# A selection-attention and ReGLU kernel: q transposed together with its selection, batch 2 moved to DMA transposes, one layout per head pair in batch 1, and earlier weights

## The chip, the cores and the metric

The kernel runs on one core of a Trainium2 chip. The metric is device time in microseconds (us); lower is better. The kernel before takes 310.8 us.

The engines are TensorE (PE in the profile; PEld is its weight loading), VectorE (DVE), ScalarE (ACT), GpSimd (POOL) and SyncE (SP). Here SyncE only starts DMA transfers, and its queue is "SPq" in the profile. The program gives every engine a list of instructions, and the traces show the list being worked through in order (two runs with the same program, before and before_dma, have TensorE's 482 groups of like matmuls in the same order). So an instruction that has to wait holds up all that stand behind it on the same engine.

## The reference

Attention in four batches of eight heads, 768 tokens, head size 64. Keys are taken in chunks of 32; each query sees only the 6 chunks with the highest upper bound of the score. A ReGLU network follows.

```python
k_min, k_max = k_chunks.min(axis=3), k_chunks.max(axis=3)          # 24 chunks of 32 keys
ub = np.sum(np.maximum(q * k_min, q * k_max), axis=-1)             # upper bound by chunk, causal
top_chunks = np.argsort(ub, axis=-1)[..., -6:]
mask = chunk_of_key_is_in_top & causal
attn = softmax(where(mask, q @ k.T / 8, -1e9)) @ v
x = attn.reshape(3072, 512)
out = (np.maximum(x @ w_gate, 0) * (x @ w_val)) @ w_out            # 512 -> 1536 -> 512
```

## The kernel before

The work is cut into 16 jobs, four pairs of heads in each of the four batches (the code counts batches b = 0 to 3, the text 1 to 4), and the feed-forward network into six units of 512 tokens. A list scheduler in Python, `Plan`, simulates the engines with assumed costs and fixes the order of instructions on each engine before anything runs. Feed-forward work of one unit fills TensorE's gaps in the attention of the next batch.

A job loads k, q and v, casts them to bf16 on GpSimd, and turns k and q so that features lie on partitions. There are two ways to do that. Batches 1 and 2 load k and q in 2-KB rows and turn them on TensorE; batches 3 and 4 load them in 256-byte rows and have SyncE start a DMA transpose:

```python
WIDE   = lambda b: b < 2     # k, q loaded in 2-KB rows
PE_KQ  = lambda b: b < 2     # k, q turned on TensorE, not by DMA transpose
PE_SEL = lambda b: b < 2     # the selection likewise
PE_X   = lambda b: b < 2     # the attention output likewise

def turned(name, tag, src, nr, on_pe, prio, after, makes, hold, np_=128):
    if on_pe:
        ...                  # nr matmuls against the identity, result in PSUM
    else:
        def f():
            t = new(tag, name, [128, nr, 128], BF16)
            nc.sync.dma_start_transpose(out=t, in_=src())
        op("SP", 1.25, prio, f, ..., lag=2.6)     # the plan's costs: 1.25 of SyncE, landing 2.6 later
```

So a job of batches 3 and 4 puts at least four transposes (k, q, selection, output) on the same in-order queue of SyncE that also starts the loads of all later jobs:

```python
# job_front(j): loads, started four jobs ahead
nc.sync.dma_start(out=o.rearrange("p (h r d) -> p h r d", h=2, d=D),
                  in_=s.rearrange("h (r p) d -> p h r d", p=128))      # rows of 256 bytes
...
# job_sel(j): the selection 0/1 per (query, chunk), turned, and copied beside q
sT = turned(sn, ..., lambda: sel, nr, on_pe, p, [("sel", j)], [sn], [])
for h in range(2):
    copy_half(eng[h], nr * 128, p + 0.01, qx[1 - h][64 * h:64 * h + 64], sT, h, ...)
# job_scores(j): 64 feature rows of k and 64 rows of a chunk indicator in one matmul of 128 rows;
# the indicator rows add a large negative number where a chunk was not selected
nc.tensor.matmul(t[:, h, o:o + m * 128], kx[h][:, c * 128:(c + 1) * 128],
                 qx[h][:, (qb - 1) * 128:(qb - 1 + m) * 128], ...)
```

Weights come through GpSimd's queue: four groups of w_gate and w_val, then four of w_out, each asked for when a certain load has landed.

The softmax here doesn't subtract the row's maximum and nothing guards it: scores larger than these inputs give would overflow.

Of the kernel before, what the change touches and what calls it, by code (L numbers as in the profile page):

```python
# [153 lines left out]
def kernel(  # L154
# [20 lines left out]


    nc = tc.nc

    B, H, S, D = q.shape
    CH = 32  # L180
    NCH = S // CH
# [21 lines left out]

    WIDE = lambda b: b < 2
    WS = 8

    PE_KQ = lambda b: b < 2
    PE_SEL = lambda b: b < 2
    PE_X = lambda b: b < 2

# [3 lines left out]

    WG = 4
    NPG = NTI // WG
    CW = NPG * 128
    wg_sb = [wpool.tile([128, KT_, CW], BF16, name=f"wg{i}") for i in range(WG)]
    wv_sb = [wpool.tile([128, KT_, CW], BF16, name=f"wv{i}") for i in range(WG)]
    wo_sb = [wpool.tile([128, NPG, d_model], BF16, name=f"wo{i}") for i in range(WG)]  # L220
    wg_h = moe_w_gate.rearrange("(kt p) n -> p kt n", p=128)
# [8 lines left out]
    sgn = const.tile([128, 2, 1], BF16)  # L230
    NSEL = 3
    sel_l = [const.tile([128, NQ, 128], BF16, name=f"sel{i}") for i in range(NSEL)]
# [7 lines left out]
    NQX = 3  # L240
    qx_l = [[const.tile([128, SQ], BF16, name=f"qx{h}_{i}") for h in range(2)]
            for i in range(NQX)]

# [27 lines left out]
    rings = {tag: n for tag, (_, _, n) in {**TAGS, **PS}.items()}  # L271
    rings["dq"] = 3
    plan = Plan(rings, set(PS))
# [15 lines left out]
    def setup():  # L289
# [3 lines left out]
        def f_sgn():  # L293
            nc.vector.memset(sgn[:, 0], -1.0)
            nc.vector.memset(sgn[:, 1], 1.0)
        op("DVE", 0.12, -99, f_sgn, makes=[("kbd0", i) for i in range(HP)])
        for i, t in enumerate(sel_l):
            op("DVE", 0.4, -98, lambda t=t: nc.vector.memset(t, 0.0), makes=[("sel0", i)])
# [22 lines left out]
        def f_i2():  # L321
# [6 lines left out]
            after=["ident2"], makes=["ind"])  # L328
        for hp in range(HP):
            for h in range(2):  # L330
                g = 64 - 64 * h
                op("DVE", 0.37, -12 + 4 * hp, lambda o=kx_l[hp][h][g:g + 64], i=ind[g:g + 64]:
                   nc.vector.tensor_copy(out=o, in_=i), after=["ind"], makes=[("kx0", hp)])


    def turned(name, tag, src, nr, on_pe, prio, after, makes, hold, np_=128):

        if on_pe:
            def f():
                t = new(tag, name, [128, nr, np_], BF16)  # L340
                s = src()
                for r in range(nr):
                    nc.tensor.matmul(t[:, r, :], s[:, r, :], ident[0:np_, 0:np_],  # L343
                                     is_transpose=True, start=(r == 0), stop=(r == nr - 1))
            op("PE", 0.057 * nr, prio, f, after=list(after) + ["ident"], makes=makes,
               take=[(tag, name)], hold=hold)
        else:
            def f():
                t = new(tag, name, [128, nr, 128], BF16)
                nc.sync.dma_start_transpose(out=t, in_=src())  # L350
            op("SP", 1.25, prio, f, after=after, makes=makes, take=[(tag, name)], hold=hold,
               lag=2.6)
        if np_ < 128:
            return lambda: TL[name].rearrange("f s p -> f p s")
        return lambda: TL[name].rearrange("f r p -> f (r p)")

    def copy_half(eng, n, prio, out, src, h, after, makes, hold):
        def f():
            i = src()[64 * h:64 * h + 64]
            if eng == "ACT":  # L360
                nc.scalar.activation(out=out, in_=i, func=ACT.Copy)
            else:
                nc.vector.tensor_copy(out=out, in_=i)  # L363
        op(eng, act_cost(n) if eng == "ACT" else dve_cost(n), prio, f, after=after,
           makes=makes, hold=hold)
# [6 lines left out]
    def first_block(b):  # L372
        p0 = -30.0 + b
        src3 = (("k", k), ("q", q), ("v", v))
        for nm, src in src3:
            rn = (nm + "raw", "P", b)

            def f_ld(nm=nm, src=src, rn=rn):
                t = new(nm + "raw", rn)
                nc.sync.dma_start(out=t[:, 0:H * D].rearrange("p (h d) -> p h d", d=D),  # L380
                                  in_=src[b, :, 0:128].rearrange("h p d -> p h d"))
            op("SP", 0.6, -40.0 + b, f_ld, makes=[("iss", nm, b - B)],
               take=[(nm + "raw", rn), ("dq", ("dq", nm, b - B))], lag=0.0)
            op("DMA", 1.22, -40.0 + b, None, after=[("iss", nm, b - B)],
               makes=[("ld", nm, b - B)], hold=[rn, ("dq", nm, b - B)])
            if nm == "v":
# [81 lines left out]
    def job_front(j):  # L468
# [8 lines left out]
        for nm, src in (("k", k), ("q", q), ("v", v)):  # L477
# [8 lines left out]
            def f_ld(nm=nm, src=src, rn=rn, np_=np_, ns=ns, lo=lo, big=big):  # L486
# [9 lines left out]
                else:  # L496
                    o = o.rearrange("p (h r d) -> p h r d", h=2, d=D)
                    for h in range(2):
                        nc.sync.dma_start(out=o[:, h],
                                          in_=s[h].rearrange("(r p) d -> p r d", p=128))  # L500
            dq = [] if big else [("dq", nm, j, i) for i in range(2)]
            op("SP", 1.1 if lo and not big else 0.6, pL, f_ld, makes=[("iss", nm, j)],
# [17 lines left out]
            def f_cast(nm=nm, rn=rn, bn=bn, np_=np_, ns=ns):  # L520
# [4 lines left out]
            op("POOL", cost, pT - 0.1, f_cast, after=[("ld", nm, j)], makes=[bn],  # L525
               take=[(nm + "bf", bn)], hold=[rn])

        on_pe = PE_KQ(b)

# [27 lines left out]
        eng = ("DVE", "DVE") if on_pe else ("ACT", "DVE")  # L557
        for h in range(2):
            copy_half(eng[h], n, pT + 0.05, tok(kx[h][64 * h:64 * h + 64]), kT, h,
                      [kn] + [("s", i) for i in prev], [("kx", j)], [kn])  # L560
        kbd = kbd_l[hp]
        for h in range(2):
            def f_kbd(h=h):
                nc.vector.tensor_tensor(
                    out=kbd[64 * h:64 * h + 64, :, 1 - h], in0=TL[mm][64 * h:64 * h + 64],
                    in1=sgn[64 * h:64 * h + 64].to_broadcast([64, 2, NCH]), op=ALU.mult)
# [9 lines left out]

        for nm, e, o in (("qmn", "ACT" if on_pe else "DVE", -1.0),
                         ("qmx", "ACT" if on_pe else "DVE", 1.0)):
            def f_q(nm=nm, e=e, o=o):
# [7 lines left out]
               makes=[("qm", j)], take=[(nm, (nm, j))], hold=[qn])  # L587
        eng = ("ACT", "ACT") if on_pe else ("ACT", "DVE")
        for h in range(2):
            copy_half(eng[h], n, pT + 0.06, tok(qx[h][64 * h:64 * h + 64]), qT, h,  # L590
                      [qn, ("s", j - NQX)], [("qx", j)], [qn])

    def job_sel(j):
# [44 lines left out]

        sel = sel_l[j % NSEL]

        def f_lt():
            nc.vector.tensor_tensor(
                out=sel.rearrange("p r (h c) -> p r h c", h=2)[:, :, :, 0:NCH],
                in0=ub(), in1=TL[tn][:, :, :, KTOP - 1:KTOP].to_broadcast([128, nr, 2, NCH]),
                op=ALU.is_lt)
        op("DVE", 0.15 + 0.0013 * nr * 2 * NCH, p, f_lt,
           after=[tn, ("sel0", j % NSEL), ("selT", j - NSEL)], makes=[("sel", j)],
           hold=[uh, tn])
        sn = ("selT", j)
        on_pe = PE_SEL(b)  # L650
        sT = turned(sn, "T" if on_pe else "tT", lambda: sel, nr, on_pe, p,
                    [("sel", j)], [sn], [])
        qx = qx_l[j % NQX]
        eng = ("DVE", "DVE") if on_pe else ("DVE", "ACT")
        for h in range(2):
            copy_half(eng[h], nr * 128, p + 0.01, qx[1 - h][64 * h:64 * h + 64], sT, h,
                      [sn, ("s", j - NQX)], [("qx", j)], [sn])

    def job_scores(j):
# [5 lines left out]
        for bi, bank in enumerate(BANKS):  # L665
# [4 lines left out]
            def f_s(bank=bank, sn=sn):  # L670
                t = new("S", sn)
                for h in range(2):
                    o = 0
                    for si, (c, qb, m) in enumerate(bank):
                        nc.tensor.matmul(t[:, h, o:o + m * 128],  # L675
                                         kx[h][:, c * 128:(c + 1) * 128],
                                         qx[h][:, (qb - 1) * 128:(qb - 1 + m) * 128],
                                         start=(si == 0), stop=(si == len(bank) - 1))
                        o += m * 128
            op("PE", 2 * w / 2400.0 + 0.02, p, f_s, after=[("kx", j), ("qx", j), ("kx0", hp)],  # L680
               makes=[sn, ("s", j)], take=[("S", sn)])
# [96 lines left out]
    def s1(u, nt, p, wide):  # L778
        hn, xn = ("hT", u), ("xT", u)
        gi, gc = divmod(nt, NPG)  # L780
        cs = slice(gc * 128, (gc + 1) * 128)
# [63 lines left out]

    def weights(key, parts, prio, after):

# [3 lines left out]
        iss = ("wi",) + key  # L851
        op("POOL", 0.78 * len(parts), prio, f, after=after, makes=[iss], lag=0.0)
        op("SDMA", 2.7 * len(parts), prio, None, after=[iss], makes=[key])

# [4 lines left out]
    offs = {}  # L859
    for j in range(NJ):  # L860
        job_front(j)
        job_sel(j)
        offs[j] = job_scores(j)
        job_av(j, offs[j])
    for i in range(WG):
        weights(("w", i), [(wg_sb[i], wg_h[:, :, i * CW:(i + 1) * CW]),
                           (wv_sb[i], wv_h[:, :, i * CW:(i + 1) * CW])],
                (-28.0, -7.9, -7.8, -7.7)[i], [(("ld","v",-1),("ld","q",0),("ld","q",1),("ld","q",2))[i]])
    for i in range(WG):
        weights(("wo", i), [(wo_sb[i], wo_h[:, i * NPG:(i + 1) * NPG, :])],  # L870
                (4.0, 5.0, 6.0, 7.0)[i], [(("ld","v",3),("ld","v",3),("ld","v",3),("ld","v",3))[i]])

# [48 lines left out]
```

## Time and profile before

| | kernel before |
|---|---|
| median of 4 runs | 310.80 us (309.11 to 311.44) |
| profiled span | 308.1 us, mean granted clock 0.972 |
| busy | PE 274.3, VectorE 184.3, ScalarE 178.1, GpSimd 91.9 us |
| last attention matmul starts | 217.3 us; then 90.8 us of feed-forward only |

From the page, the span in 40 slices of 7.7 us. A digit is the busy share of a slice in tenths; PEclk is the granted clock, DMA the mean busy share of the 16 DMA engines.

```profile
PE   2841998967998998999999899999999999999994
PEclk9995899995999999999999999999999999999999
DMA  9999999999899779986662264231100110020002
```

TensorE is the limit from about 130 us to the end. It is not before: it waits around slices 3 and 4 and around slice 9, and its clock drops to a half after each of these waits. The DMA engines are full for the first ten slices and begin to have room at about 80 us.

The windows view of the kernel before, in three stretches: start and end, length, then busy us (and instructions) of PE, PEld, DVE, ACT and POOL, then granted clock, DMA share and GB/s.

```profile
0.00:80.00 80.00, 56.09 (x521) 32.29 (x530) 50.85 (x150) 39.69 (x53) 40.54 (x68) 0.89 1.20 210
80.00:200.00 120.00, 114.56 (x1128) 66.66 (x1146) 104.53 (x327) 99.09 (x131) 47.28 (x88) 1.00 0.72 139
200.00:308.10 108.10, 103.64 (x585) 49.53 (x593) 28.89 (x49) 39.30 (x60) 4.03 (x11) 1.00 0.12 41
```

TensorE is idle for 24 us of the first 80, but for only 5.4 us of the next 120. A DMA share above 1 is an artefact of overlapping records; read it as full.

The waits view names the transfers that it waited for (us in total, times, longest):

```profile
PE g L793 <- DMA wg_61<-in_moe_w_gate_dram: 6.0, 1, 6.0
PE yp L828 <- DMA wo_69<-in_moe_w_out_dram: 2.6, 1, 2.6
PE yp L828 <- DMA wo_70<-in_moe_w_out_dram: 2.2, 1, 2.2
```

The timeline of SyncE's queue, cut to six lines (start, length, queue, line, operation). The length is how long the instruction held the queue, not how long the transfer took. The time in which the queue waits for a producer is the pause before a line, as the 5.6 us before 107.04:

```profile
84.36 1.05 SPq L499 DMA_DIRECT2D qraw<-in_q_dram  x2
85.51 0.48 SPq L494 DMA_DIRECT2D vraw<-in_v_dram  x1
...
99.01 1.31 SPq L350 DMA_TRANSPOSE kT<-kbf  x1
100.38 1.06 SPq L494 DMA_DIRECT2D kraw<-in_k_dram  x1
107.04 0.94 SPq L499 DMA_DIRECT2D qraw<-in_q_dram  x2
108.03 1.21 SPq L350 DMA_TRANSPOSE qT<-qbf  x1
```

When nothing is in the way, a plain load holds the queue about 0.5 us and a transpose about 1.2 us.

### The profile page before, as it was taken

Reading aid. Unit: us, or ns where it says so; the run is one execution under the profiler, and the core shown is the slowest. Engines: PE = TensorE matmul, PEld = TensorE weight load, DVE = VectorE, ACT = ScalarE, POOL = GpSimd, SP = SyncE. Lnnn points to the kernel's source line nnn. Section 1 sums busy time; section 2 is a strip of 40 time slices with the busy share of each in tenths; the row PEclk is TensorE's granted clock in tenths of the full one; section 3 lists DMA queues with packets and bytes.
Section 4 is the critical chain, followed back from the end, with each engine's and each line's share of the span. In section 5 each row is a group of like instructions: output and inputs, shape, how many; then the busy total and the mean of one; then the engine's idle time right before and its main releaser. Section 6 shows DMA issues by size and latency. Waiting matters only on the chain.

```text
span 308.1 us, 5930 instructions
## 1 busy us (share of the span) xinstructions
PE 274.3 (89%) x2230; PEld 148.5 (48%) x2268; DVE 184.3 (60%) x524; ACT 178.1 (58%) x242; POOL 91.9 (30%) x164
## 2 busy tenths in 40 slices
PE   2841998967998998999999899999999999999994
PEld 1431455643565554555655455555544444444441
DVE  7454789952879999978998798523434023204310
ACT  3421378860979794877898788988233223233321
POOL 5594146670555263243533332223000000000000
PEclk9995899995999999999999999999999999999999
DMA  9999999999899779986662264231100110020002
GB/s 168 218 229 222 212 214 227 209 187 231 158 235 242 90 172 186 187 145 137 168 139 49 56 89 80 92 80 54 24 0 0 69 70 0 34 104 1 0 34 102
DMA packets 95389, 37.88 MB, mean 123 GB/s; under 512 B 83840, under 2 KB 89472, under 8 KB 95360
## 3 DMA queue, kind: packets, MB, share of 16 engines
q1 hardware_dynamic: 89536, 32.78, 53.5%
q0 software_dynamic: 5824, 4.72, 9.6%
q8 instruction: 17, 0.28, 0.4%
q14 instruction: 12, 0.10, 0.1%
HBM read 30.41 MB, written 6.29 MB: 119 GB/s over the span
## 4 chain that ended last, share of the span: by engine, by line
PE 58%; DMA 19%; POOL 6%; DVE 5%; issue 5%; ACT 3%; SPq 2%; POOLq 0%; ACTq 0%; DVEq 0%
PE g L793 20%; PE yp L828 19%; DMA vraw<-in_v_dram 7%; PE sT L675 7%; PE vl L793 6%; PE o L726 5%; DMA kraw<-in_k_dram 5%; DMA wo_70<-in_moe_w_out_dram 3%; DMA qT<-qbf 2%; DMA kT<-kbf 2%; POOL aT L698 2%; DVE kmm L552 1%; SPq L380 1%; ACT aT L686 1%; POOL kbf L521 1%
## 5 line engine op out<-in xcount | busy, mean ns | idle before, releaser
L686 ACT ACTIVATE aT<-sT 128x1024 bf16<-128x1024 f32 x80 | 78.7, 1022 | 20.7 <-PE sT L675 16.7
L804 ACT ACTIVATE grl<-g 128x512 bf16<-128x512 f32 x72 | 42.9, 596 | 58.5 <-PE g L793 50.3
L698 POOL TENSOR_SCALAR_AFFINE_SELECT aT<-aT 128x256 bf16<-128x256 bf16 x80 | 32.2, 417 | 63.5 <-ACT aT L686 63.1
L812 DVE TENSOR_TENSOR hT<-vl,grl 128x512 bf16<-128x512 f32 x48 | 33.1, 689 | 21.3 <-PE vl L793 20.2
L828 PEld LDWEIGHTS <-hT 128*128 128x128 bf16 x288 | 27.7, 99 | 37.2 <-issue 3.8
L812 DVE TENSOR_TENSOR hT<-g,grl 128x512 bf16<-128x512 f32 x24 | 16.6, 692 | 45.3 <-ACT grl L804 31.6
L552 DVE TENSOR_REDUCE kmm<-kT 128x24 bf16<-128x768 bf16 x32 | 29.8, 948 | 7.4 <-PE kT L343 7.2
L838 ACT ACTIVATE y<-yp 128x512 f32<-128x512 f32 x24 | 14.4, 598 | 27.3 <-PE yp L828 23.3
L675 PEld LDWEIGHTS <-kx_all 128*128 128x128 bf16 x256 | 21.5, 98 | 14.3 <-issue 1.3
L726 PEld LDWEIGHTS <-aT 128*128 128x128 bf16 x640 | 23.2, 98 | 9.3 <-POOL aT L698 2.7
L793 PE MATMUL g<-xT,wg_61 128*128 128x512 bf16 x69 | 18.5, 390 | 6.1 <-DMA wg_61<-in_moe_w_gate_dram 6.0
L828 PE MATMUL yp<-wo_69,hT 128*128 128x512 bf16 x71 | 19.9, 386 | 3.0 <-DMA wo_69<-in_moe_w_out_dram 2.6
L828 PE MATMUL yp<-wo_70,hT 128*128 128x512 bf16 x70 | 20.3, 400 | 2.2 <-DMA wo_70<-in_moe_w_out_dram 2.2
L828 PE MATMUL yp<-wo_71,hT 128*128 128x512 bf16 x70 | 19.2, 379 | 0.2
L828 PE MATMUL yp<-wo_72,hT 128*128 128x512 bf16 x70 | 19.0, 379 | 0.1
L793 PE MATMUL g<-xT,wg_63 128*128 128x512 bf16 x70 | 18.2, 379 | 0.9 <-ACT grl L804 0.8
L521 POOL CAST kbf<-kraw 96x1024 bf16<-96x1024 f32 (+1 forms) x16 | 15.2, 952 | 11.6 <-DMA kT<-kbf 5.1
L363 DVE COPY kx_all<-kT 64x768 bf16<-64x768 bf16 x24 | 18.2, 759 | 0.4
L793 PE MATMUL g<-xT,wg_62 128*128 128x512 bf16 x70 | 18.2, 379 | 0.2
L793 PE MATMUL g<-xT,wg_64 128*128 128x512 bf16 x69 | 18.2, 379 | 0.1
L521 POOL CAST qbf<-qraw 80x1024 bf16<-80x1024 f32 (+1 forms) x16 | 14.1, 882 | 13.4 <-DMA qT<-qbf 11.5
L741 DVE TENSOR_TENSOR x<-o,zr 128x320 bf16<-128x320 f32 x32 | 15.7, 491 | 1.1
(187 smaller groups left out, 449.7 us busy)
## 6 DMA issues: line engine op xcount, KB each, us to landing
kraw<-in_k_dram SPq DMA_DIRECT2D x16, 384.0 KB, 7.6
vraw<-in_v_dram SPq DMA_DIRECT2D x16, 384.0 KB, 6.4
out_dram<-y SPq DMA_DIRECT2D x24, 256.0 KB, 2.0
qraw<-in_q_dram SPq DMA_DIRECT2D x8, 320.0 KB, 12.2
qraw<-in_q_dram SPq DMA_DIRECT2D x16, 160.0 KB, 3.7
kraw<-in_k_dram SPq DMA_DIRECT2D x4, 256.0 KB, 5.0
qraw<-in_q_dram SPq DMA_DIRECT2D x4, 256.0 KB, 5.0
vraw<-in_v_dram SPq DMA_DIRECT2D x4, 256.0 KB, 5.1
```

The costliest lines, as they stand in the source:

```text
L363: nc.vector.tensor_copy(out=out, in_=i)
L521: nc.gpsimd.tensor_copy(out=new(nm + "bf", bn)[0:np_, 0:ns * 2 * D].rearrange("p (r h d) -> p r h d", h=2, d=D), in_=TL[rn][0:np_, 0:ns * ...
L552: nc.vector.tensor_reduce(out=TL[mm][:, m], in_=i, axis=AX.XY if wide else AX.X, op=o)
L675: nc.tensor.matmul(t[:, h, o:o + m * 128], kx[h][:, c * 128:(c + 1) * 128], qx[h][:, (qb - 1) * 128:(qb - 1 + m) * 128], start=(si == 0), ...
L686: nc.scalar.activation(out=TL[an][:, :, a0:a0 + w], in_=TL[sn][:, :, 0:w], func=ACT.Exp, scale=scale)
L698: nc.gpsimd.affine_select(out=d, in_=d, compare_op=ALU.is_ge, fill=0.0, base=0, channel_multiplier=-1, pattern=[[0, 2], [1, 128]])
L726: nc.tensor.matmul(TL[on][:, r - 1, h - h0, :], TL[an][:, h, o:o + 128], vb[:, h, c, :], start=(i == 0), stop=(i == NP - 1))
L741: nc.vector.tensor_tensor(out=TL[xn][:, :, h0 * D:(h0 + hs) * D].rearrange("p r (h d) -> p r h d", d=D), in0=TL[on][:, :, :, 0:D], in1=TL[ ...
L793: nc.tensor.matmul(ps, w[:, kt, cs], TL[xn][:, kt, :], start=(kt == 0), stop=(kt == KT_ - 1))
L804: nc.scalar.activation(out=new("grl", rn), in_=g, func=ACT.Relu)
L812: nc.vector.tensor_tensor(out=TL[hn][:, nt, :], in0=vv, in1=TL[rn], op=ALU.mult)
L828: nc.tensor.matmul(TL[pn], TL[hn][:, nt, tl * 128:(tl + 1) * 128], wo_sb[nt // NPG][:, nt % NPG, :], start=(nt == 0), stop=(nt == NTI - 1))
```

## The change

The change aims at TensorE's idle first 80 us, and at work that TensorE and VectorE need not do. It has four parts:

- **W** (weights): the first group of w_gate and w_val is smaller (groups of 2, 3, 3 and 4 columns of 128), all are asked for earlier, w_out comes in two halves, v loads of the first blocks are put back, and the plan allows more loads under way.
- **P** (pair): in batch 1 both heads of a pair share one layout, so that copies from PSUM become single copies of all 128 partitions; the scores become pairs of 64-row matmuls.
- **D** (DMA): batch 2 gives up its TensorE transposes and its 2-KB rows and is treated as batches 3 and 4.
- **J** (join): GpSimd casts q a second time, in token order, into a tile beside the selection; one DMA transpose of that tile delivers the score operand, where before the selection was transposed alone and four half copies followed.

The diff, cut to its core (comments after # are added here; "..." marks cuts):

```diff
@@ weights: four groups, the first smaller; w_out in two halves
-    WG = 4
-    NPG = NTI // WG
+    WGS = [2, 3, 3, 4]
+    NPG = NTI // 2                      # w_out's halves
-    rings["dq"] = 3
+    rings["dq"] = 6                     # loads that the plan lets be under way
@@ ... weights asked for when loads are issued, not when they have landed
-                (-28.0, -7.9, -7.8, -7.7)[i], [(("ld","v",-1),("ld","q",0),("ld","q",1),("ld","q",2))[i]])
+                (-28.0, ...)[i], [(("iss","v",-1),("iss","k",0),("iss","v",0),("iss","v",1))[i]], 1.5 if i == 0 else 3.5)
@@ batch 2 joins batches 3 and 4: 256-byte rows and DMA transposes
-    WIDE = lambda b: b < 2
+    WIDE = lambda b: b < 1
+    PAIR = lambda b: b < 1
-    PE_KQ = lambda b: b < 2
-    PE_SEL = lambda b: b < 2
-    PE_X = lambda b: b < 2
+    PE_KQ = lambda b: b < 1
+    PE_SEL = lambda b: b < 1
+    PE_X = lambda b: b < 1
@@ q and its selection side by side in token order, one tile
-    qx_l = [[const.tile([128, SQ], BF16, ...) for h in range(2)] for i in range(NQX)]
+    qx_l = [const.tile([128, NQ, 2, 128], BF16, name=f"qx{i}") for i in range(NQX)]
+    cb_l = [const.tile([128, NQ, 2, 128], BF16, name=f"cb{i}") for i in range(NCB)]
+            if nm == "q" and not PAIR(b):
+                def f_cb(cb=cb, rn=rn):                      # GpSimd, besides the cast to qbf
+                    for h in range(2):
+                        nc.gpsimd.tensor_copy(out=cb[:, :, h, h * D:h * D + D], in_=src[:, h])
@@ ... one transpose in place of two copies of qT, one transpose and two copies of selT
+            op("SP", 1.6, p, lambda: nc.sync.dma_start_transpose(
+                out=qx.rearrange("f r h p -> f (r h) p"),
+                in_=cb.rearrange("p r h c -> p (r h c)").rearrange("p (x c) -> p x c", c=128)),
+               after=[("sel", j), ("cbq", j), ("s", j - NQX)], makes=[("qx", j), ("cT", j)],
+               lag=2.6 + 0.7)
@@ batch 1: one layout for both heads of a pair, scores as pairs of 64-row matmuls
+                if PAIR(b):
+                    for k_, q_, first in ((kx[0], x[:, 0:SQ], True), (ind, x[:, SQ:], False)):
+                        for si, (c, qb, m) in enumerate(bank):
+                            for h in range(2):
+                                hs = slice(64 * h, 64 * h + 64)
+                                nc.tensor.matmul(t[:, h, o:o + m * 128],
+                                                 k_[hs, c * 128:(c + 1) * 128],
+                                                 q_[hs, (qb - 1) * 128:(qb - 1 + m) * 128], ...)
```

## The prediction

> **What bounds the kernel now.** Span 308.1 us, TensorE (PE) busy 274.3. By stretch (windows view): 0–30.2 us, PE 12.8 busy; 30.2–71.4, 35.0 of 41.2; 71.4–133.8, 58.4 of 62.4; 133.8–218, 82.3 of 84.2; 218–308, 85.8 of 90.1. So PE is the limit from about 130 us on. Before that it waits: 6.0 us for the first gate-weight group (asked for at 16.8 us, landed 12.9 us later, first FFN matmul at 30.2), 2.6 + 2.2 us for w_out near 70 us (waits view), and runs cold after both (granted clock 0.63 in 20–30, 0.66 in 70–80). DMA moves 187–212 GB/s until 134 us; VectorE is 85% busy in 71–134.
>
> **What the change does, costed.**
> 1. Weights: first group 2/3 as large, all asked for before the jobs' first kbf cast. Both tensors of the old first group took 15.4 us from the ask; two thirds of that from an ask at about 14 us gives 24–25 us (estimate): first FFN matmul about 5 us earlier, w_out no longer late. Cost: loads share the DMA engines with more weight traffic (the Trainium skill, "DMA: Bandwidth & Descriptors", section "Issuing engines are not separate DMA queues"; the trace agrees: weights take 13–19 us to land beside the loads).
> 2. Batch 2 loses 104 PE transposes (a job: kT 0.51, qT 0.45, xt 0.44, selT alike, drain included): about 5 us of PE.
> 3. Batch 1 scores: twice as many matmuls, of 64 rows, in pairs on both halves. The first-block scores, 8 such of 128 columns, took 0.40 us, as much as 4 full ones: pairs overlap, as the Trainium skill's "TensorEngine Tiling (Array Packing)", "Key Properties", says; it also says a mode switch drains. 40 switches, estimate 1–3 us of PE.
> 4. VectorE: batch 1 saves a 0.96 and a 0.48 us copy a job; batch 2 kx copies (1.92, now one of 0.36), sel copies (0.96), xT copies (about 1.1); batches 3 and 4 about 1.0 a job. About 25 us less of 184. ScalarE: about 13 less. GpSimd: about 10 more (q cast twice).
> 5. DMA: 20 more transposes in batch 2 where DMA is saturated, joined ones twice as large, batch-2 k and q loads in 256-byte rows instead of 2 KB. Estimate 25–35 us more DMA work, against 0.57 free in 134–218.
>
> **What lies on the critical path.** Early weights 5 us plus about 2 at w_out; PE work −5 +2; relief of VectorE in 71–134 perhaps 3, given back in part by transposes behind loads in the congested stage (kT and qT landings of 5 us are already in the chain at 112–130). The last 90 us (pure FFN) don't change. Sum about −10 us.
>
> **Predicted: 300.5 us**, 80% range 291.5 to 309. Faster by over 2%: 0.70; within 2%: 0.26; slower: 0.04.
>
> **What would show each step.** First FFN matmul (g) at 24–26 us, its DMA wait below 3; first yp at 61–66 instead of 71.4, no wait over 1 us for w_out; PE busy 268–273; VectorE 155–162, ScalarE 162–168, GpSimd 100–105; attention's last matmuls at about 208 instead of 218; FFN tail still 90 us.
>
> **What would make it wrong.** Job 0's k cast now stands behind all weight issues on GpSimd, its k load behind two q loads: if that slips to 30 us, PE, in order, gains nothing early. Transposes of batch 2 stuck in SP's queue behind stalled loads (issues stall up to 8.7 us now) would starve PE at 70–110. If the 64-row pairs don't overlap, PE gets 8.5 us more. Conversely, with both weight waits gone and the clock full, 290 is possible.

## More of the kernel before

All times quoted are medians of a kernel's runs, all in the fast state unless the text says otherwise; ratios use fast runs alone.

The DMA view gives the median time from the start of a transpose to its landing, the last number:

```profile
kT<-kbf SPq DMA_TRANSPOSE x8, 3.4
qT<-qbf SPq DMA_TRANSPOSE x8, 2.6
```

## The result, and the profile after

The changed kernel is correct and slower: 320.56 us (319.55 to 321.17, 4 runs). The ratio is 1.032, with a 95% interval of 1.027 to 1.037. Ratios in this document are the mean time of one kernel's fast runs over that of the other's of the same rounds, so they are not quite the ratio of the medians quoted. The medians of the kernel before differ a little (308.97 to 310.81 us), so each experiment is judged by its own ratio.

The same views of the changed kernel. The slices (7.9 us each):

```profile
PE   2937999999579759698969989999999999999995
PEclk9985999999869859889989999999999999999999
DMA  9999999999999999999889642142000020020002
```

The windows:

```profile
0.00:80.00 80.00, 65.35 (x660) 35.94 (x670) 51.55 (x162) 43.83 (x59) 41.99 (x75) 0.94 1.23 208
80.00:200.00 120.00, 100.07 (x898) 54.98 (x911) 80.77 (x256) 76.86 (x100) 51.22 (x100) 0.90 0.97 172
200.00:317.90 117.90, 113.31 (x638) 54.15 (x647) 30.91 (x61) 42.15 (x65) 5.14 (x13) 1.00 0.14 44
```

Two things happened. In the first 80 us TensorE is busy 65.35 us instead of 56.09: the early weights work as intended. In the next 120 us it is busy 100.07 instead of 114.56, at a mean clock of 0.90 instead of 1.00, while the DMA share rises from 0.72 to 0.97. The gain is 9.3 us and the loss 14.5 us. The last attention matmul starts at 227.1 us instead of 217.3, and from there both kernels take 90.8 us to the end. So the whole difference of the two spans, 9.8 us, has arisen by then. Batch 2's attention is not what ends later (its exponentials end at 136.1 us, 140.0 before); what falls behind is the feed-forward work that should fill its gaps: by 140 us the trace shows 213 feed-forward matmuls started, against 246 before (of 864; both traces lack some records). PEclk falls again in the middle of the span; each drop follows one or more waits. The Trainium skill, "TensorE: Matmul & The Clock Gate", section "HAM oscillation — how this bites in real kernels", says that waits for DMA which outlast a window of about 3.4 us put the clock back to its slow state. Here the waits for DMA were up to 3.6 us and the clock was 0.74 in 100 to 120 us, where it had been 1.00 before; but drops also followed waits of 2.6 and 2.3 us for ScalarE (before 132.2 and 162.9 us).

The waits view of TensorE no longer lists any weight. In its place:

```profile
PE sT L727 <- DMA qx_91<-cb_94: 5.1, 2, 3.6
PE sT L727 <- DMA qx_92<-cb_95: 3.9, 2, 3.6
```

These are joined transposes of batch 2 (and, for 1.5 of the 9.0 us, of batch 3), waited for by the score matmuls. The chain of work that ended last, between 82 and 115 us, its DMA pieces (start, length, what):

```profile
82.94 6.37 DMA qx_92<-cb_95
...
96.45 4.03 DMA vraw<-in_v_dram
100.48 4.11 DMA kT<-kbf
...
110.09 4.30 DMA qx_91<-cb_94
```

The chain runs through transfers here, while the chain of the kernel before runs through TensorE and VectorE in 83 to 109 us. SyncE's queue, at the time of the first of these waits:

```profile
82.94 2.78 SPq L690 DMA_TRANSPOSE qx_92<-cb_95  x1
...
87.20 3.53 SPq L362 DMA_TRANSPOSE qT<-qbf  x1
90.94 1.21 SPq L362 DMA_TRANSPOSE kT<-kbf  x1
92.19 1.42 SPq L514 DMA_DIRECT2D qraw<-in_q_dram  x2
93.74 1.23 SPq L362 DMA_TRANSPOSE qT<-qbf  x1
...
171.99 0.53 SPq L895 DMA_DIRECT2D out_dram<-y  x1
```

It goes from one instruction to the next: from 82 to 172 us no pause is longer than 0.45 us, while the kernel before has 14 pauses over 0.5 us there, 29.8 us in all. So in this stage the producers are ready whenever the changed kernel's queue reaches an entry, and the queue sets the pace. Some transposes hold it 2.8 or 3.5 us instead of 1.2. Added up over stretches of 20 us, instruction by instruction from the trace (plain transfers + transposes, in us held of 20):

| stretch | before | after |
|---|---|---|
| 60–80 | 18.8 + 0 | 12.2 + 5.2 |
| 80–100 | 11.0 + 1.0 | 7.0 + 11.3 |
| 100–120 | 4.3 + 6.6 | 4.9 + 13.8 |
| 120–140 | 8.4 + 3.3 | 5.4 + 13.3 |
| 140–160 | 2.5 + 10.6 | 5.6 + 13.1 |
| 160–180 | 0 + 12.5 | 4.0 + 14.5 |

Before, the queue is held 11 to 13 us of each 20 from 80 us on. After, it is held 17.4 to 18.7 us of each 20 for 120 us; the rest are the short steps from one instruction to the next. Landings of transposes lengthen too:

```profile
kT<-kbf SPq DMA_TRANSPOSE x12, 4.2
qT<-qbf SPq DMA_TRANSPOSE x12, 3.9
qx_91<-cb_94 SPq DMA_TRANSPOSE x4, 3.9
```

The plan had assumed 2.6 us (3.3 for the joined one).

### The profile page after: what moved, and what is told of

Same layout as the page of the kernel before. It is cut to its first block, busy times and chain, and to the rows that moved or that the text cites. A ratio compares the mean times of both kernels' runs of the same rounds, so it can differ in the third digit from the quotient of the medians.

```text
span 317.9 us, 5858 instructions
## 1 busy us (share of the span) xinstructions
PE 278.7 (88%) x2193; PEld 145.1 (46%) x2228; DVE 163.2 (51%) x478; ACT 162.8 (51%) x222; POOL 98.4 (31%) x186
## 2 busy tenths in 40 slices
DMA packets 124348, 42.59 MB, mean 134 GB/s; under 512 B 114208, under 2 KB 119840, under 8 KB 124320
## 4 chain that ended last, share of the span: by engine, by line
PE 61%; DMA 22%; SPq 5%; ACT 4%; DVE 3%; issue 2%; POOL 2%; ACTq 0%; DVEq 0%
PE g L846 23%; PE yp L881 15%; PE vl L846 9%; DMA kraw<-in_k_dram 6%; PE sT L727 6%; DMA kT<-kbf 6%; PE o L779 4%; DMA qx_91<-cb_94 3%; DMA qx_92<-cb_95 3%; DMA vraw<-in_v_dram 3%; ACT aT L739 2%; SPq L394 2%; PE sT L717 1%; DVE hT L865 1%; SPq L514 1%
## 5 line engine op out<-in xcount | busy, mean ns | idle before, releaser
L881 PE MATMUL yp<-wo_69,hT 128*128 128x512 bf16 x140 | 36.1, 390 | 0.2
L881 PE MATMUL yp<-wo_70,hT 128*128 128x512 bf16 x137 | 34.5, 382 | 0.5 <-issue 0.2
L727 PEld LDWEIGHTS <-kx_all 128*128 128x128 bf16 x192 | 17.2, 102 | 30.0 <-issue 17.9
L846 PE MATMUL g<-xT,wg_64 128*128 128x512 bf16 x92 | 24.6, 383 | 0.2
L536 POOL CAST kbf<-kraw 128x768 bf16<-128x768 f32 (+1 forms) x16 | 14.3, 895 | 25.9 <-DMA kT<-kbf 11.4
L727 PE MATMUL sT<-qx_92,kx_all 128*128 128x512 bf16 (+3 forms) x64 | 12.8, 334 | 9.1 <-ACT aT L739 5.2
L846 PE MATMUL g<-xT,wg_63 128*128 128x512 bf16 x69 | 19.0, 393 | 1.4 <-ACT grl L857 1.1
L536 POOL CAST qbf<-qraw 128x640 bf16<-128x640 f32 (+1 forms) x16 | 13.1, 821 | 17.6 <-DMA qraw<-in_q_dram 12.9
L846 PE MATMUL g<-xT,wg_62 128*128 128x512 bf16 x67 | 18.2, 379 | 0.3
L375 ACT ACTIVATE kx_all<-kT 64x768 bf16<-64x768 bf16 x12 | 10.1, 842 | 15.9 <-DMA kT<-kbf 15.9
L846 PE MATMUL vl<-xT,wv_68 128*128 128x512 bf16 x61 | 17.2, 396 | 0.2
L610 ACT ACTIVATE qmn<-qT 128x640 bf16<-128x640 bf16 x16 | 11.7, 734 | 10.3 <-DMA qT<-qbf 6.8
L727 PE MATMUL sT<-qx_91,kx_all 128*128 128x512 bf16 (+3 forms) x64 | 11.8, 316 | 5.1 <-DMA qx_91<-cb_94 5.1
```

The lines of the kernel that those rows point to most:

```text
L536: nc.gpsimd.tensor_copy(out=new(nm + "bf", bn)[0:np_, 0:ns * 2 * D].rearrange("p (r h d) -> p r h d", h=2, d=D), in_=TL[rn][0:np_, 0:ns * ...
L610: nc.scalar.activation(out=tok(t), in_=qT(), func=ACT.Relu, scale=o)
L727: nc.tensor.matmul(t[:, h, o:o + m * 128].rearrange("k (r p) -> k r p", p=128), kx[h][:, c * 128:(c + 1) * 128], qx[:, qb - 1:qb - 1 + m, ...
L846: nc.tensor.matmul(ps, w[:, kt, cs], TL[xn][:, kt, :], start=(kt == 0), stop=(kt == KT_ - 1))
L881: nc.tensor.matmul(TL[pn], TL[hn][:, nt, tl * 128:(tl + 1) * 128], wo_sb[nt // NPG][:, nt % NPG, :], start=(nt == 0), stop=(nt == NTI - 1))
```

## The experiments

18 kernels ran. All ran 3 rounds. The main theory and its rivals:

1. **D loses the time**, because batch 2's transposes queue up behind loads on SyncE while the DMA engines are full.
2. W loses it: weights asked for early delay the loads.
3. J loses it: twice as many bytes in a transpose, or the second cast on GpSimd.
4. P loses it: 64-row matmuls do not pay.
5. The rows of 256 bytes lose it, not the transposes.

A sixth was not named: the plan is built anew for each kernel, so a part that is changed can also change the order of work on every engine. The traces show where it did; it is said below where it matters.

### One part at a time

**w_only**: the kernel before with W.

```diff
-    WG = 4
+    WGS = [2, 3, 3, 4]
-    rings["dq"] = 3
+    rings["dq"] = 6
     ... (w_out in halves, earlier asks, as in the change)
```

> The kernel before with the weight part of the change alone (group sizes 2, 3, 3, 4, earlier asks, two w_out halves, the order of the first-block loads). Theory 1 (the loss is batch 2's move from PE to DMA transposes, while the DMA engines are saturated): this alone gains, about 302 us, first yp near 62 us instead of 71. Theory 2 (the join is the loss): the same, about 302. Theory 3 (the early weights push the loads of batches 1 and 2 back and the loss comes from there): about 316 or more.

Measured: 312.58 us, ratio 1.012 (1.005 to 1.019). TensorE is busy 61.6 us in 0 to 80 (56.1 before), but 50.8 in 80 to 140 (56.3 before): it gains 5.5 us and gives 5.5 back. Feed-forward unit 0 is done at 89.1 instead of 96.5 us, but batch 2's exponentials end at 140.5 instead of 140.0. What was done early was the filler work that TensorE had for the later gaps; the pace there is set by how fast batch 2 gets ready. So the early gain was real and not kept; that it was lost in this way is read from these times and not tested by itself. The main theory had expected about 302 us here: that was wrong.

**d_only**: the kernel before with D.

```diff
-    WIDE = lambda b: b < 2        # and PE_KQ, PE_SEL, PE_X
+    WIDE = lambda b: b < 1
```

> The kernel before with batch 2 handed to DMA transposes and 256-byte loads, as batches 3 and 4 have it, and nothing else. Theory 1: slower than before, 320 to 328 us, PE idle between 80 and 180 us. Theory 2 (join): within 2% of before, about 309, as there is no joined transpose in it. Theory 3: within 2% of before.

Measured: 319.65 us, ratio 1.034 (1.030 to 1.039). D alone costs as much as the whole change. TensorE is busy 46.4 us in 80 to 140, where it was 56.3 before, and SyncE's queue goes through 82 to 172 us with only one pause over 0.5 us (1.1), as in the changed kernel.

**no_move**: the changed kernel with batch 2 back on TensorE, in the pair layout (W + P + J).

```diff
-    WIDE = lambda b: b < 1        # and PAIR, PE_KQ, PE_SEL, PE_X
+    WIDE = lambda b: b < 2
```

> The changed kernel with batch 2 given back to PE (wide loads, PE transposes, one layout per pair in batches 1 and 2); weights early and join in batches 3 and 4 stay. Theory 1: faster than both kernels, about 299 us. Theory 2: the join is still in 8 of 12 jobs, so about two thirds of the loss stays: 311 or more. Theory 3: 315 or more.

Measured: 311.2 us, ratio 1.006 (1.001 to 1.012). Without D, 2.5 of the 3.2 per cent are gone. The theory had expected about 299 us, faster than both kernels: the rest of the change gains nothing either. The parts do not add up (1.2 for W, 3.4 for D, 0.8 for P and J below, 3.2 together). The run also shows how 64-row matmuls run. Its timeline of TensorE (start, length, line, operands):

```profile
51.16 0.39 PE L717 MATMUL sT<-qx,kx_all 64*128 64x512 bf16 x2
51.39 0.38 PE L717 MATMUL sT<-qx,ind 64*128 64x512 bf16 x2
51.60 0.38 PE L717 MATMUL sT<-qx,kx_all 64*128 64x512 bf16 x2
51.82 0.38 PE L717 MATMUL sT<-qx,ind 64*128 64x512 bf16 x2
```

Each line is two matmuls, one on each half of the rows, and the next pair starts 0.21 to 0.23 us later. So pairs do overlap, and twice the number of matmuls takes about the same time. In the chain, four such matmuls take 0.54 us where two full ones take 0.43, and twelve 0.55 where six take 0.44: about 0.1 us for each of the five banks of a job, so about 0.5 us a job. This agrees with the Trainium skill, "TensorEngine Tiling (Array Packing)", section "Key Properties", that tiles work independently; that the extra 0.1 us is the drain of which it speaks is not shown.

**pair_join**: the kernel before with P in batches 1 and 2 and J in 3 and 4.

```diff
 # the no_move kernel with the parts of W taken back:
-    WGS = [2, 3, 3, 4]
+    WG = 4
-    rings["dq"] = 6
+    rings["dq"] = 3
```

> The kernel before with one layout per pair in batches 1 and 2 and the join in batches 3 and 4, without the weight part and without the move of batch 2. The runs so far put the weight part at +1.2% and the weight part with this at +0.6%: if the parts add up, 0.6% faster than before, 307 to 309 us. If VectorE's relief is worth what I predicted (3 us or more): 303 to 306.

Measured: 312.15 us, ratio 1.008 (1.004 to 1.011). Both expectations (307 to 309, 303 to 306) were missed: VectorE's relief gained nothing that shows.

**join_only**: the kernel before with J in batches 3 and 4.

```diff
+    JOIN = lambda b: b >= 2
-            if nm == "q" and not PAIR(b):
+            if nm == "q" and JOIN(b):        # second cast of q, by GpSimd
```

> The kernel before with the join in batches 3 and 4 alone (batches 1 and 2 in the old layout on PE, old weight groups). These batches had slack on the DMA engines (0.34 to 0.67 busy), and VectorE and ScalarE lose about 1 us a job each. If that relief counts: 1 to 2% faster than both kernels, 304 to 307 us. If PE has other work to do meanwhile: within 0.5% of before.

Measured: 314.7 us, ratio 1.013 (1.007 to 1.020). The wait of the attention-value matmuls for GpSimd's masking, 1.6 us in the kernel before, is here

```profile
PE o L791 <- POOL aT L763: 4.3, 5, 1.5
```

and GpSimd is busy 19.8 us of 140 to 180 instead of 15.8, TensorE 35.4 instead of 38.4. GpSimd works in order as well, so that the second cast of q stands before the masking of an earlier job. That this is the cause is argued from these numbers; no run took the cast alone away. Neither expectation (1 to 2 per cent faster, or within 0.5 per cent) came true.

**no_join**: the changed kernel without J.

```diff
-            if nm == "q" and not PAIR(b):
+            if False:
     ... (selection transposed alone, q and selection copied in halves, as before)
```

> The changed kernel without the join: q's and the selection's own DMA transposes and four half copies, as batches 3 and 4 had before; early weights, pair layout and batch 2 on DMA stay. Theory 1: still slow, 317 to 325 us. Theory 2: fast, about 303. Theory 3: about 318.

Measured: 318.56 us, ratio 1.032 (1.027 to 1.038), but the result was wrong (relative error 0.084): batch 1 and the other batches used different blocks of the same tile for the chunk bounds, so that stale blocks stayed in it. The instructions are the same as in the mended version.

**no_join2**: the same with a tile of bounds of its own for batch 1.

```diff
-    kbd_l = [const.tile([128, 2, 2, NCH], BF16, ...) for i in range(HP)]
+    kbd_l = [const.tile([128, 2, 2, NCH], BF16, ...) for i in range(2 * HP)]
```

> The changed kernel without the join, as no_join, with a zeroed tile of its own for batch 1 so that the result is right; the same instructions otherwise. Theory: the join plays no part in the loss, so again 317 to 322 us.

Measured: correct, 319.05 us, ratio 1.031 (1.027 to 1.036), the same as with J (1.032). So rival 3 does not explain the loss of the changed kernel, although J alone, on the kernel before, costs 1.3 per cent.

### What it is about D

**narrow_only**: the kernel before with only the rows of batch 2's k and q cut to 256 bytes, still turned on TensorE.

```diff
-    WIDE = lambda b: b < 2
+    WIDE = lambda b: b < 1
```

> The kernel before, with batch 2's k and q loaded in 256-byte rows instead of 2 KB ones, and batch 2 still transposed on PE. The move of batch 2 alone cost 3.4%; this does the load half of it. If the 256-byte rows are what costs (DMA engines' time per packet): 317 us or more. If the 20 DMA transposes cost it: within 1% of before, 308 to 312 us.

Measured: 310.85 us, ratio 1.010 (0.997 to 1.023), unclear: four of the seven runs of the kernel before in this call were slow, which leaves three to compare with (the same holds for d_poolq, before_wide and w_wide). By the interval it is at most two thirds of D's loss: rows alone do not make it.

**d_poolq**: d_only, with the loads of batches 2 to 4 started by GpSimd, to free SyncE's queue for the transposes.

```diff
+                qu = nc.gpsimd if b else nc.sync
-                    nc.sync.dma_start(...)
+                    qu.dma_start(...)
```

> Batch 2 on DMA transposes in the kernel before (which cost 3.4%), with the plain q, k and v loads of batches 2 to 4 asked for by GpSimd, so that SP's queue holds only transposes, first loads and stores. The DMA engines get the same work. If transposes wait because SP's one queue is full and in order: most of the loss comes back, 309 to 313 us. If the DMA engines' throughput is the limit: 317 us or more (GpSimd pays about 0.75 us an ask, so it may be slower still).

Measured: 343.01 us. Two of the four runs, the profiled one among them, were slow; the two fast ones give 1.105 (1.084 to 1.126). GpSimd is busy 134.9 us instead of about 92; what limits this kernel was not taken apart. It says nothing about SyncE's queue.

**before_wide, w_wide, after_wide**: three kernels with all 256-byte loads of the jobs in contiguous rows of 1,280 or 1,536 bytes per partition instead. Tokens land in the wrong places, so the results are wrong; the instructions, their order on every engine, and the bytes are the same.

```diff
-                                      in_=s.rearrange("h (r p) d -> p h r d", p=128))
+                                      in_=s.rearrange("h (p r) d -> p h (r d)", p=128))
```

> The kernel before with every 256-byte-row load of the jobs (v of all batches, k and q of batches 3 and 4) read in rows of 1280 or 1536 bytes: same bytes, same instructions, a fifth to a sixth of the packets; tokens land in other places, so the result is wrong on purpose. If DMA throughput holds the first 100 us back: 2% or more faster, 300 to 304 us. If VectorE and the dependence chains hold it: within 1% of before.

> The weights-only kernel (1.2% slower than before) with the same wide rows, wrong on purpose too. If its early gain of 6 us at the end of batch 1 was lost to late batch-2 loads (DMA throughput): 298 to 303 us and at least 1% faster than the wide kernel before. If it was lost to VectorE's chains or to the order of work: still 1% slower than the wide kernel before.

> The changed kernel with all its 256-byte-row job loads read in rows of 1280 or 1536 bytes (same bytes and instructions, far fewer packets; wrong result on purpose). If batch 2's transposes starve PE because the DMA engines are full of small packets: DMA landings of kT, qT and the joined one fall towards 2.6 us and the time to 308 us or less. If the transposes' own length and SP's in-order queue are what costs: 315 us or more.

Measured: before_wide 308.11 us, ratio 1.004 (0.987 to 1.021), unclear (one of its runs was slow; it is in the median and left out of the ratio); w_wide 309.61 us, 1.005 (0.995 to 1.015), unclear; after_wide 309.59 us, 0.999 (0.994 to 1.004). So wide rows give the changed kernel its whole loss back, and give the kernel before nothing that can be seen. w_wide is not faster than before_wide, so it does not show that W's gain was lost to late loads; the intervals are too wide for more. The windows of after_wide:

```profile
0.00:80.00 80.00, 63.72 (x618) 34.32 (x618) 52.01 (x146) 41.09 (x55) 41.65 (x73) 0.91 0.99 206
80.00:200.00 120.00, 110.61 (x1060) 61.89 (x1059) 86.78 (x289) 85.79 (x112) 53.91 (x106) 0.97 0.83 182
```

TensorE has 110.61 us in the middle stretch, against 100.07 in the changed kernel. The same 42.59 MB moved in 76,220 packets instead of 124,348. In the first 80 us the rate was the same (206 and 208 GB/s) at a DMA share of 0.99 instead of 1.23. That fits the Trainium skill, "DMA: Bandwidth & Descriptors", section "Specifications", which puts the smallest transfer for full rate at 512 bytes: the changed kernel has 114,208 packets under that, this one 55,840. SyncE's queue and the landings in after_wide:

```profile
82.83 1.35 SPq L690 DMA_TRANSPOSE qx<-cb  x1
...
160.85 0.54 SPq L895 DMA_DIRECT2D out_dram<-y  x1
```

```profile
kT<-kbf SPq DMA_TRANSPOSE x12, 4.6
qT<-qbf SPq DMA_TRANSPOSE x12, 4.1
qx<-cb SPq DMA_TRANSPOSE x12, 4.1
```

The transposes land no sooner than in the changed kernel, and yet the time is back. So the latency of a transpose is not what is lost, and neither of the two expectations fits. What differs is when a transfer gets its turn. SyncE's order is the same in both kernels, so the queue can be compared entry by entry. In the first 60 us it is held 19.3 us, against 56.3 in the changed kernel, and loads come early; but that lead is not kept, since batch 2's first transpose starts at 68.1 us, after a pause of 21 us, and in the changed kernel at 63.7. At 82.8 and 82.9 us both kernels stand at the same joined transpose. The 73 entries from there to the same store (160.85 above, 171.99 in the changed kernel) take 78.0 us here and 89.1 there, without a pause over 0.45 us in either. That is 11.0 of the 11.1 us by which the two spans differ (306.8 and 317.9). The queue is as full in one as in the other, but its entries let go sooner: the 35 transposes hold it 51.5 us instead of 57.9, and the 38 plain transfers 20.3 instead of 24.9. Batch 2's exponentials end at 128.0 us instead of 136.1.

**after_lag**: the changed kernel, with a plan that assumes 2 us more until a transpose has landed.

```diff
-               lag=2.6)           # and 2.6 + 0.7 for the joined one
+               lag=4.6)
```

> The changed kernel, its schedule built with 4.6 us assumed from a transpose's issue to its landing instead of 2.6 (measured: 3.6 to 4.2 median); no work changes, only the order of the instructions on each engine. If the loss is a static order that asks too early for late transposes: 305 to 312 us. If the stage has too little throughput: within 1% of the changed kernel, 317 to 323.

Measured: 320.86 us, ratio 1.037 (1.033 to 1.041). A plan with a truer latency, which puts much of the work in another order, is no better. It agrees with after_wide that the latency is not the point.

**after_pex**: the changed kernel with the attention output of batch 2 turned on TensorE, as before; 8 transposes fewer on SyncE.

```diff
-    PE_X = lambda b: b < 1
+    PE_X = lambda b: b < 2
```

> The changed kernel with the transposes of x of batch 2 back on PE (8 of batch 2's 20 DMA transposes, about 2.5 us of SP's queue a job; 20 PE transposes more). If SP's queue time is the limit in 80 to 180 us: a third or more of the loss comes back, 313 to 316 us. If it is the DMA engines' throughput: about a fifth of the bytes added, so 318 or so. If VectorE were the limit (it gets the copies back): no gain, 320 or more.

Measured: 317.26 us, ratio 1.024 (1.021 to 1.028). Taking 8 of the 20 added transposes (the output's, which few wait for at once) off the queue gives back 0.8 of the 3.2 per cent: less than the third that was expected if the queue is the limit, and near the 318 us that was expected if DMA throughput is.

**before_sp**: the kernel before, with three tiny loads (1 KB each, into a scratch tile) on SyncE at each of the 20 places where D would put a transpose, behind the same producers. TensorE still does the transposes, so that nothing waits for these loads.

```diff
+        if JOBS[j][0] == 1:
+            tiny(j, prio_of(j, "T"), [("kbf", j)])
+            tiny(j, prio_of(j, "T") + 0.03, [("qbf", j)])
+            tiny(j, prio_of(j, "U"), [("sel", j)])
+            tiny(j, prio_of(j, "X"), [("x", j)])
+            tiny(j, prio_of(j, "X"), [("x", j)])
```

> The kernel before, with three loads of 1 KB each on SP's queue in the places where each of batch 2's 20 transposes would stand (60 in all, about 1.2 us of SP's time per place), behind the same producers; next to no bytes; the result is right. If SP's in-order queue is what the transposes cost: 316 to 320 us. If the DMA engines' time is: within 1% of before, 308 to 312.

Measured: 320.45 us, ratio 1.035 (1.031 to 1.038). SyncE's timeline and the middle window:

```profile
104.33 1.48 SPq L600 DMA_DIRECT2D scr<-in_q_dram  x3
```

```profile
80.00:200.00 120.00, 104.63 (x1018) 61.20 (x1034) 94.16 (x287) 87.25 (x114) 41.81 (x77) 0.96 0.68 132
```

A group of three holds the queue about as long as one transpose, and moves 60 KB in all. The DMA share of the middle stretch is even lower than in the kernel before (0.68, 0.72), and still TensorE loses 9.9 us there. Batch 3's first transpose gets its turn at 101.56 us instead of 99.01, and TensorE then waits 5.1 us for ScalarE, which waits for that transpose. One thing was not held fixed: the plan was built with the new entries, and from about 150 us on the order of work on the other engines differs in places (64 of TensorE's 482 groups of matmuls). Up to there the order is that of the kernel before, and TensorE is already 6.2 us late. So time on SyncE's queue in these places, behind these producers, is enough by itself for a loss of about 6 us; in the rest the new order may share.

**before_dma**: the kernel before, with 16 extra loads of 192 KB in 256-byte rows into a scratch tile in batch 2: DMA traffic, with 16 issues on SyncE instead of 60.

```diff
+        if JOBS[j][0] == 1:
+            more(j, prio_of(j, "T"), [("kbf", j)])         # 4 a job
+            ...
```

> The kernel before with four more loads of 192 KB in 256-byte rows a job in batch 2 (3.1 MB in all, what the 20 transposes move or somewhat more), into a scratch nobody reads, behind the same producers. If the DMA engines' time is what the transposes cost: 315 us or more. If SP's queue is (16 issues of some 0.4 to 1 us against 20 of 1.2 to 3.5): 310 to 313.

Measured: 316.15 us, ratio 1.021 (1.017 to 1.025). The order of work on the other engines is that of the kernel before throughout. Batch 3's first transpose gets its turn at 103.11 us, and TensorE waits 5.4 us behind it, as in before_sp. The 16 loads held the queue nearly as much as the 60 tiny ones did (49.3 us of 80 to 140, against 50.7 in before_sp and 34.5 before), so this run does not show traffic apart from the queue.

**after_actv, before_actv**: the v loads of batches 2, 3 and 4 (12 loads) started by ScalarE's queue, everything else and the planned order as they were.

```diff
+                    eng = nc.scalar if nm == "v" and b >= 1 else nc.sync
-                    nc.sync.dma_start(out=o.rearrange("p (h r d) -> p h r d", h=2, d=D),
+                    eng.dma_start(out=o.rearrange("p (h r d) -> p h r d", h=2, d=D),
```

> The changed kernel with one word altered: the v loads of the jobs of batches 2, 3 and 4 (12 loads) are issued by ScalarE's queue instead of SyncE's; the planned order of every engine stays. Theory (SyncE's queue time starves the changed kernel between 80 and 190 us): the 12 loads hold SyncE at least 0.6 us each and up to 8 us when stalled, so the share of SyncE held in 60 to 120 us falls, attention ends earlier by 3 to 8 us, ratio to before 1.005 to 1.02 (the changed kernel had 1.03). Rival (it is the DMA engines' traffic that delays the transposes, and the queue's holding is only a symptom): same bytes, same rows, so the ratio stays 1.03 or above. A third outcome: ScalarE itself is held by stalled issues as SyncE was, its exponentials come late, and the ratio rises above 1.04 with ScalarE named in the waits; then the run says nothing on the rival.

> The kernel before with the same one alteration. Theory: SyncE holds its queue full only until about 105 us there and TensorE's limits after 134 us are its own work, so little changes: ratio 0.985 to 1.005. If ScalarE is held by the stalled issues: above 1.01. It is also the version most likely to beat the kernel before.

Measured: after_actv 318.84 us, ratio 1.026 (1.020 to 1.032); before_actv 318.57 us, 1.023 (1.015 to 1.032; one of its four runs was slow, the median of the other three is 317.72). Both expectations of the theory fail: the first is above the 1.005 to 1.02 that was named, with an interval that takes in both the theory's upper end and the changed kernel's ratio; the second should have stayed below 1.005. ScalarE was hardly held; its queue in after_actv:

```profile
93.73 0.39 ACTq L510 DMA_DIRECT2D vraw<-in_v_dram  x1
```

But SyncE's queue filled up again: in 80 to 160 us it was held 73.9 us, against 74.3 in the changed kernel. A queue without pauses is held all the time whatever stands in it, so the pace has to be looked at. Between the two entries used for after_wide, nine v loads were gone; the stretch took 84.8 us instead of 89.1, and the queue was 4.0 us ahead at its end. The 29 plain transfers left there held it 22.5 us, more each (0.78) than the 38 of the changed kernel (0.66). So the number of entries counts, and how fast the DMA engines take them counts as well. This fits the first half of what the Trainium skill, "DMA: Bandwidth & Descriptors", section "Issuing engines are not separate DMA queues", says, that transfers interleave on the same 16 engines whoever starts them. The lead was lost again: a kT transpose that started at 165.3 us, 2.6 us earlier than in the changed kernel, landed at 171.3, only 0.6 us earlier, and TensorE waited 4.6 us behind it; why it took 6.0 us was not taken apart. In before_actv the loads of batch 2 ran ahead, SyncE was held only 1.0 us of 60 to 80 (18.8 before), and w_out came late: TensorE waited 6.0 us for it, against 4.8 before, and its first w_out matmul came at 72.0 (68.4 before), stopping again for 1.6 us before 75.05. Batch 2's exponentials ended at 149.9 us instead of 140.0. Here the early loads for the attention lost more than they gained; that the late weights are the reason is read from these times.

## Why the prediction was wrong

The prediction said 300.5 us (291.5 to 309) and "faster by over 2%" at 0.70. It was 320.56 us, slower by 3.2 per cent, to which it had given 0.04. Point by point:

| predicted | measured | |
|---|---|---|
| first FFN matmul (g) at 24–26 us | 26.5 (30.2 before) | just outside |
| its DMA wait below 3 us | no such wait | right |
| first yp at 61–66 | 61.5 (68.4 before; the 71.4 of the prediction is the second w_out group's) | right |
| no wait over 1 us for w_out | none | right |
| PE busy 268–273 | 278.7 | wrong: the clock was 0.946 instead of 0.972; from these, about 34 us instead of 17 ran at half clock, which can add up to about 8 us (estimate) |
| VectorE 155–162, ScalarE 162–168, GpSimd 100–105 | 163.2, 162.8, 98.4 | just outside, right, just outside |
| 64-row pairs overlap, 1–3 us in all | they do; about 0.5 us a job, so 2 us | right |
| attention's last matmuls at about 208 | 227.1 (217.3 before) | wrong by 19 us |
| FFN tail still 90 us | 90.8, as before | right |

The removed and added work was counted well on every engine but one. Three terms of the sum failed:

1. **"5. DMA: 20 more transposes in batch 2 ..."** This was costed as work of the DMA engines alone, and held against the free DMA share of 134 to 218 us. Batch 2's scores run from about 90 to 140 us, and its operands are made from about 70 us on, where there was less room, and the transposes also need time on SyncE's queue: 20 × 1.2 us at best, behind loads in the same order. This is the step that failed: the path had SyncE's queue in it, and the sum did not. The critical-path sum gave it no number ("given back in part by transposes behind loads"). Measured, D alone costs 3.4 per cent, about 10 us; from 82 to 172 us the queue goes on without a pause over 0.45 us, where it had paused 29.8 us before, and TensorE waits 9.0 us for joined transposes, 7.5 of them in batch 2. The paragraph on what would make it wrong named this, "Transposes of batch 2 stuck in SP's queue behind stalled loads ... would starve PE at 70–110", and then gave it next to no weight in the range (0.04 for any slower result).
2. **"Early weights 5 us plus about 2 at w_out"** was counted as time kept. W made TensorE 5.5 us busier in the first 80 us and cost the same 5.5 us in 80 to 140, since it spent the filler work early; the whole of W was 1.2 per cent slower.
3. **"relief of VectorE in 71–134 perhaps 3"** did not come. VectorE is busy 21 us less over the span, but in the middle stretch batch 2's operands come from SyncE and the DMA engines, and VectorE has 80.77 us of work in 120 us there.

What is shown of the cause: D makes the loss (d_only, no_move). J does not (no_join2), narrow rows alone do not (narrow_only), a transpose's latency does not (after_wide, after_lag). The changed kernel's new order of work does not either: after_wide has the same order on every engine and loses nothing. From 82 to 172 us SyncE's queue sets the pace of the changed kernel, and the whole gain of after_wide is made there, by entries that let go of the queue sooner. SyncE's time at these places is enough for a loss of about 6 us with next to no traffic (before_sp). The reading that fits all of these is that each of the two needs the other: a queue in strict order, full of loads that leave at the pace of busy DMA engines, into which 20 further entries are put that attention waits for.

What stays open is the split between the two. before_sp and before_dma each put a load on the kernel before, both of them on its queue, and neither is exactly D. The direct test, relieving the queue with the traffic unchanged (after_actv), put the queue 4.0 us ahead and lost this again. after_wide lightens the traffic and, with it, the queue. For the smaller losses, W's gain and its return are read from the busy times of two stretches; J's cause is only argued.

No correct kernel that ran beats the kernel before. The nearest with any of the change's intent in it is no_move, 0.6 per cent slower.

## What to carry to other kernels

Before moving work from a busy engine to DMA transfers, add up the time that the starting queue will be held in that very stage, at the held times that the trace shows under load, as one would for a compute engine. To see whether a queue sets the pace, look for its pauses, and compare two kernels with the same order entry by entry; a share of time held in a fixed stretch says little once there are no pauses. Work that fills gaps is only a gain if the gaps are still open later: ask which wait ends last after the gain, not how much earlier something starts. If a named risk is one that the trace already shows in part (issues held up to 8.7 us), it belongs in the sum with a number.

## What the Trainium skill lacked or had wrong

- "DMA: Bandwidth & Descriptors", section "Issuing engines are not separate DMA queues", says that starting DMAs from several engines saves only sequencer time, "usually small relative to the DMA itself". Here it was not small: 60 loads of 1 KB on SyncE's queue made the kernel 3.5 per cent slower (before_sp, about 6 us of it in an unchanged order of work), while the DMA share fell from 0.72 to 0.68 in the stretch. Its first half, that transfers share the same engines, fits after_actv.
- No page that was read says how long a plain start or a transpose holds SyncE's queue under load. Here a transpose held it 1.2 us with room and up to 3.5 us without, and a plain load about 0.4 to 0.5 us on SyncE with room, and without up to 8.7 us in the kernel before and 10.5 in the changed one; the v loads held ScalarE's queue 0.37 to 0.44 us in after_actv, and once 4.06 us in before_actv.
- "DMA: Bandwidth & Descriptors", section "DMA Transpose (X-bar)", gives rules for use but no time to landing. Here it was 2.4 to 3.4 us (median by tile) in the kernel before and up to 4.2 in the changed one, and 4.6 for kT in after_wide, where the kernel was faster.
- "TensorEngine Tiling (Array Packing)", section "Key Properties", says that a change of mode drains, without a size. Here each bank of two pairs of 64-row matmuls took about 0.1 us more than full ones (no_move); that this is the drain is not shown.
- "SBUF — State Buffer", section "SBUF: two separate sides", says that a VectorE operation with two inputs in SBUF can be blocked by a GpSimd operation that reads SBUF. It has no figure for small operations; in no_move two of 64x48, usually 0.42 us together, took 3.70 us while GpSimd was busy, one of them 3.32. That GpSimd's reads blocked it is not shown.
